# A recurrence kernel with a planned instruction order: an opening loaded in another order, with fewer filler products, a drain in place of a copy, and new planner numbers

## The chip, the cores and the metric

The kernel runs on one core of one Trainium2 chip. The metric is device time in microseconds (us) of one execution of the whole program. Besides TensorE (PE, with its weight loads as PEld), VectorE (DVE), ScalarE (ACT) and GpSimd (POOL) the core has SyncE (SP), which here issues nearly all DMAs, in order.

## The reference

Three stages follow one another. The first is a gated recurrence over 768 steps for 4 batches of 8 heads of 48, the other two mix the result by token and by channel.

```python
f = 1.0 / (1.0 + np.exp(-f_logit))
for t in range(S):
    state = f[:, :, t, :, None] * state + np.einsum('bhd,bhe->bhde', k[:, :, t], v[:, :, t])
    y[:, :, t] = np.einsum('bhd,bhde->bhe', q[:, :, t], state)
...
h = gelu_tanh(x @ w_in); u, v = halves of h
v_n = layernorm(v) * g_ln
v_s = np.einsum('ts,bsd->btd', w_sg, v_n) + b_sg[None, :, None]
x = x + (u * v_s) @ w_out
...
theta = x @ w_theta
y = einsum('ts,bsd->btd', w_tok_r, x * cos(theta)) + einsum('ts,bsd->btd', w_tok_i, x * sin(theta))
u = x + y
out = u + np.maximum(u @ w_ch, 0.0)
```

## The kernel before

The recurrence is cut into chunks of 64 tokens. For each batch the 768 tokens are two halves of 384, and each half has four units of two heads. The last unit of a half is put together from rows of the first three by small DMAs (`qkv3<-qkv0` and so on), so it can start only when those three have been scaled.

A half begins with the logits: ACT makes the gate from them, DVE runs a scan along the tokens, ACT makes the inverse of the running product. For batch 0 this is done in three parts of 384 columns, one for each of the first three units; for the later batches in one piece of 1152. GpSimd fills the scan's second operand (`seed`) and clears the last unit's tile by memsets. Then DVE scales K and Q of each unit (`scaled`). A unit (`unit`) has, on PE: three transposes of K (L822), updates and scores (L834, L843), the product inside a chunk (`inner`, L925), and the product with the state carried from earlier chunks (`carried`, L980; later batches do both in one, L940). Between them DVE masks the scores (`am`) and chains six small state steps (L871 to L880), with ACT scaling some of them (L885). ACT then copies the result to `y` (L911), and SP moves it into `xst` (L902), from which the dense part reads.

In batch 0 the first of the `carried` products reads its second block of state from spare columns of `am`; ACT puts it there by a copy (L972) that waits for the state.

The dense part of the first batch begins with plain fp32 products (`mm1`, L1014) on weights that DVE and ACT decode from 64-bit inputs (L534 to L537, `early`). Later products are three fp32r products each (`mm3`, L1002 to L1004). Batch 0's dense part is interleaved with batch 1's recurrence, and so on.

The order on every engine comes from a planner (`Plan.schedule`). It plays the operations through with costs written into the code, picks among those that are ready the one with the smallest due time (`vt`), and emits the instructions in that order; each engine then runs its list strictly in order. Constants at the top set due times: `LATE` says by when batch 1's recurrence is spread over batch 0's dense part, `U_AT` when a part of the first weights is due, `EVEN` and `ODD` when weights are decoded for later. Where the planner sees PE without work before `WARM_TO`, it puts in filler products on `ident` (L1382); how many is fixed when the program is built. On the chip they run in PE's list like any other product: 26 products are 52 records in the trace, since each fp32 product shows as two pieces.

Of the kernel before, what the change touches and what calls it, by code (L numbers as in the profile page):

```python
# [8 lines left out]
F32 = mybir.dt.float32  # L9
# [8 lines left out]
P = 128  # L18
# [41 lines left out]
EVEN, ODD = (0.05, 0.5), (0.9, 0.4)  # L60
# [3 lines left out]
LATE = 75.0  # L64
HF0, HF1, V_AT, U_AT, DENSE = (-60.0, -38.0), (-44.0, -16.0), -46.0, -24.0, -35.0
# [3 lines left out]
YQ = "SP"  # L69
MQ = "SP"  # L70
# [7 lines left out]
TICK = 10.24 / 3  # L78
DMA_SLACK = 1.0
# [60 lines left out]
class Plan:  # L140
# [63 lines left out]
    def schedule(self):  # L204
# [4 lines left out]
        free = {e: 0.0 for e in LAT}  # L209
        ticks = {}  # L210
# [39 lines left out]
        def run(a, dur, left):  # L250

            c, i = left / dur, int(a / TICK + 1e-9)
            while left > 1e-6:
                rate = c if ticks.get(i - 1, 0) >= 3060 else c / 2
                n = min(left, rate * ((i + 1) * TICK - a))
                ticks[i] = ticks.get(i, 0) + n
                left, a, i = left - n, a + n / rate, i + 1
            return a
# [99 lines left out]
def body(tc, ctx, att, lat, qkv, flog, w_in, g_ln, w_sgT, b_sg, w_out, w_theta, w_rT, w_iT, w_ch, out):  # L358
# [37 lines left out]
    gate = const.tile([P, 1], F32, name="gate")  # L396
    halfpi = fill("halfpi", math.pi / 2)
# [113 lines left out]
    def a1(n):  # L511
        return 0.1 + n * 0.00081
# [157 lines left out]
    first, ends = Buf(), []  # L670
# [12 lines left out]
    def half(pl, g, b, hf, xst, carry, vt, step):  # L683
# [15 lines left out]
        later = [first] if b else []  # L699
        for p, (t, root) in enumerate(tiles):  # L700
            for p0, p1 in groups:
                if p0 == p:
                    dma(
                        pl, eng, P * (p1 - p0) * TH * 4,
                        lambda gp=slice(p0, p1): q[eng].dma_start(f.t[:, gp], flog[b, hf][:, gp]), later, wp=fp[p0:p1],
                    )
            if p == NT:
                moved, vb, clear = (Buf(of=root) for _ in range(3))
                pl.op("POOL", 0.1 + QKE * 0.0008, lambda t=t: nc.gpsimd.memset(t.t[:, :QKE], 0.0), w=[clear], vt=vt)
# [11 lines left out]
        for p0, p1 in groups:  # L721
            gp, fs, ss, n = slice(p0, p1), fp[p0:p1], sp[p0:p1], (p1 - p0) * TH
            if b == 0:

                pl.op("POOL", 0.1 + n * 0.0008, lambda gp=gp: nc.gpsimd.memset(seed.t[:, gp], 2.0**62), w=ss)
# [11 lines left out]
                pl.op("DVE", 0.03 + n * 0.00214, scan, r=ss, w=fs)  # L737
                pl.op("ACT", a1(n), lambda gp=gp: A(seed.t[:, gp], f.t[:, gp], AF.Ln), r=fs, w=ss, table="L")
# [66 lines left out]
    def unit(pl, g, b, hf, p, be, bb, t, parts, xst, carry):  # L805
# [42 lines left out]
        if before:  # L848
            r, w, dur, fn = before
            pl.op("PE", 0.25 + 0.1 * nu + dur - 0.12, lambda fn=fn: (fn(), scores()), r=[kb, qb, vb, kt, *r], w=[ps, *w], small=True)  # L850
            carry.pop("out")()
        else:
            pl.op("PE", 0.25 + 0.1 * nu, scores, r=[kb, qb, vb, kt], w=[ps], small=True)
# [76 lines left out]
        if fused:  # L930
# [27 lines left out]
            if hf == 1 and p == NP - 1:  # L958
                r, w, dur, fn = both_
                pl.op("PE", dur, fn, r=r, w=w, small=True)  # L960
# [5 lines left out]
        def apart():  # L966
            pl.op("PE", 0.5, inner, r=[vb, am], w=[ps], small=True)
            late = range(1 - hf, 2 * NC2)
            turn = [(c, j) for c in late for j in range(2)]
            c0 = late[0]  # L970
            behind = lambda: am.t[wide[1], 1, (NC2 - 1) * HP : (NC2 - 1) * HP + D]
            pl.op("ACT", 0.2, lambda: nc.scalar.copy(behind()[:D], S[c0][0]()[rows[1]]), r=[S[c0][1]], w=[am])  # L972
            turn.remove((c0, 1))
            turn.insert(0, (c0, 1))

            def carried():
                for c, j in turn:
                    i, a = halves[c]
                    moved = (c, j) == turn[0]
                    nc.tensor.matmul(  # L980
                        score(a, i)[rows[j]], behind()[:D] if moved else S[c][0]()[rows[j]], Q()[rows[j], tok(i, a)], start=False,
                        stop=i == NC2 - 1,
                    )

            pl.op("PE", 0.134 * len(late), carried, r=[qb, *(S[c][1] for c in late), am], w=[ps], small=True)
# [631 lines left out]
```

## Time and profile before

| what | value |
|---|---|
| runs | 592.37, 595.15, 598.02 us; median 595.15 |
| profiled execution, its own time | 594.94 us |
| its span, first to last instruction | 593.2 us |
| busy share of the span | PE 97%, PEld 89%, DVE 80%, ACT 63%, POOL 4% |
| chain that ended last | PE 72%, DVE 11%, ACT 8%, DMA 5% |

The span is 1.7 us less than the execution's time. The profiled execution lies within 0.3 us of the median. A busy engine is not always one at work that the result needs: in the first 36 us much of PE's busy time is filler products. The last matmul begins 586.58 us after the span's start; what follows is one residual step and the last stores.

### The profile page before, as it was taken

What the parts mean: (1) busy time and instruction counts of PE and PEld (TensorE: products, weight loads), DVE (VectorE), ACT (ScalarE), POOL (GpSimd) and SP (SyncE); (2) the same over time, 40 slices, a digit from 0 to 9 for tenths busy, and PEclk for the clock granted to TensorE, in tenths of its full rate; (3) what the DMA queues carried; (4) which work ended last, traced back from release to release, by engine and by line L of the source; (5) the groups of instructions that cost most, each with busy time, mean ns of one, the idle gap of its engine ahead of it and who ended that gap; (6) DMA issues with size and microseconds to landing.
All of it is one profiled execution on the core that took longest, in us unless ns stands there. A gap on an engine that the chain in (4) does not pass through costs nothing.

```text
span 593.2 us, 14971 instructions
## 1 busy us (share of the span) xinstructions
PE 572.7 (97%) x5767; PEld 528.7 (89%) x5767; DVE 473.8 (80%) x1127; ACT 374.0 (63%) x828; POOL 24.8 (4%) x38
## 2 busy tenths in 40 slices
PE   8889999989999999999999999999999999999995
PEld 8646687978799989999999998999999999999995
DVE  5987789999789998699886777999968459898542
ACT  5869998569795668957488335785344249553410
POOL 3002000011001010000000000000000000000000
PEclk9999999999999999999999999999999999999999
DMA  8669574878787799787899898366788745548612
GB/s 284 177 190 306 190 216 139 283 221 251 233 278 255 255 286 329 229 247 208 275 319 328 286 330 310 125 211 231 247 273 265 249 142 158 162 135 252 187 41 85
DMA packets 61295, 136.26 MB, mean 230 GB/s; under 512 B 8096, under 2 KB 28320, under 8 KB 61216
## 3 DMA queue, kind: packets, MB, share of 16 engines
q1 hardware_dynamic: 61216, 135.23, 70.5%
q8 instruction: 47, 0.77, 0.6%
q14 instruction: 32, 0.26, 0.1%
HBM read 93.90 MB, written 34.21 MB: 216 GB/s over the span
## 4 chain that ended last, share of the span: by engine, by line
PE 72%; DVE 11%; ACT 8%; DMA 5%; issue 2%; SPq 1%; POOL 0%; DVEq 0%; ACTq 0%; POOLq 0%
PE mm L1002 16%; PE mm L1004 15%; PE mm L1003 15%; PE lmm L1004 5%; PE lmm L1002 5%; PE lmm L1003 5%; PE mm L1382 2%; DMA xst<-y 2%; PE at L940 2%; ACT L346 2%; PE at L925 1%; PE at L843 1%; PE at L822 1%; PE at L834 1%; DVE tmp L1083 1%
## 5 line engine op out<-in xcount | busy, mean ns | idle before, releaser
L1002 PE MATMUL mm<-st,ar 128*128 128x384 f32 x192 | 67.0, 349 | 0.9 <-ACT tmp L1204 0.6
L1004 PE MATMUL mm<-st,ar 128*128 128x384 f32 x192 | 64.5, 336 | 0.2 <-DVE ar L1238 0.2
L1003 PE MATMUL mm<-st,ar 128*128 128x384 f32 x192 | 64.2, 334 | 0.0
L1036 ACT CAST early<-xst 128x384 fp32r<-128x384 f32 x42 | 21.4, 511 | 30.6 <-DVE xst L1041 23.2
L1002 PEld LDWEIGHTS mm<-st,ar 128*128 128x128 f32 x192 | 36.0, 188 | 2.8 <-ACT tmp L1204 0.9
L1296 ACT CAST wout<-ar 128x384 fp32r<-128x384 f32 x48 | 24.2, 511 | 19.5 <-PE lmm L1003 9.6
L1004 PEld LDWEIGHTS mm<-st,ar 128*128 128x128 f32 x192 | 36.0, 188 | 0.5 <-DVE ar L1238 0.5
L1003 PEld LDWEIGHTS mm<-st,ar 128*128 128x128 f32 x192 | 36.1, 188 | 0.4 <-issue 0.2
L1002 PE MATMUL mm<-ar,wout 128*128 128x384 f32 x96 | 33.7, 351 | 1.7 <-DVE tmp L1128 1.3
L1002 PE MATMUL mm<-early,win 128*128 128x384 f32 x102 | 35.1, 345 | 0.0
L1004 PE MATMUL mm<-early,win 128*128 128x384 f32 x102 | 34.2, 336 | 0.0
L1003 PE MATMUL mm<-early,win 128*128 128x384 f32 x102 | 34.2, 335 | 0.0
L1003 PE MATMUL mm<-ar,wout 128*128 128x384 f32 x96 | 32.5, 338 | 0.9 <-DVE ar L1025 0.9
L1004 PE MATMUL mm<-ar,wout 128*128 128x384 f32 x96 | 32.2, 336 | 0.0
L1297 DVE TENSOR_TENSOR wout<-ar,wout 128x384 fp32r<-128x384 f32 x48 | 25.5, 551 | 7.3 <-ACT wout L1296 7.2
L1002 PE MATMUL mm<-win,early 128*128 128x512 f32 (+1 forms) x78 | 30.8, 394 | 0.0
L1004 PE MATMUL mm<-win,early 128*128 128x512 f32 (+1 forms) x78 | 29.4, 376 | 0.3 <-DVE early L1037 0.3
L1003 PE MATMUL mm<-win,early 128*128 128x512 f32 (+1 forms) x78 | 29.3, 375 | 0.0
L1041 DVE TENSOR_TENSOR xst<-xst,mm 128x384 f32<-128x384 f32 x42 | 22.5, 548 | 7.9 <-PE mm L1004 7.7
L346 ACT ACT_TABLE_LOAD x19 | 24.4, 1283 | 1.1 <-PEq L1609 0.8
L1041 DVE TENSOR_TENSOR xst<-xst,lmm 128x384 f32<-128x384 f32 x30 | 15.7, 549 | 11.8 <-PE lmm L1004 11.8
L1037 DVE TENSOR_TENSOR early<-xst,early 128x384 fp32r<-128x384 f32 x42 | 22.4, 551 | 2.2 <-ACT early L1036 2.1
(304 smaller groups left out, 1812.8 us busy)
## 6 DMA issues: line engine op xcount, KB each, us to landing
st<-scratch SPq DMA_DIRECT2D x76, 384.0 KB, 4.0
scratch<-wt SPq DMA_DIRECT2D x48, 384.0 KB, 4.1
lst<-scratch SPq DMA_DIRECT2D x44, 384.0 KB, 3.8
qkv<-in_qkv SPq DMA_DIRECT2D x21, 538.0 KB, 5.6
scratch<-st SPq DMA_DIRECT2D x12, 384.0 KB, 3.6
raw<-in_w_rT SPq DMA_DIRECT2D x12, 384.0 KB, 6.0
raw<-in_w_iT SPq DMA_DIRECT2D x12, 384.0 KB, 5.3
out<-xst SPq DMA_DIRECT2D x24, 192.0 KB, 2.2
```

The costliest lines, as they stand in the source:

```text
L346: self.nc.scalar.preload_act_table_set(SETS[load])
L822: nc.tensor.transpose(ps.t[:, 0, c], K()[:, c], ident)
L940: nc.tensor.matmul(o[rows[j]], state_[rows[j]], Q()[rows[j], tok(i, a)], start=False, stop=i == NC2 - 1 and a == 1,)
L1002: nc.tensor.matmul(o, h0, h1, start=start, stop=False, skip_group_check=more)
L1003: nc.tensor.matmul(o, h0, l1, start=False, stop=False, skip_group_check=more)
L1004: nc.tensor.matmul(o, l0, h1, start=False, stop=stop, skip_group_check=more)
L1036: pl.op("ACT", a1(TH), lambda: nc.scalar.copy(Xh(), T()), [src], [hi])
L1037: pl.op("DVE", v1(TH), lambda: V.tensor_sub(Xl(), T(), Xh().bitcast(F32)), [src, hi], [lo])
L1041: pl.op("DVE", v1(TH), lambda: V.tensor_add(T(), T(), ps.t[:, :TH]), [ps], [xst[hf].parts[k]])
L1296: pl.op("ACT", a1(TH), lambda: nc.scalar.copy(f.t[:, 0], st()), [sb], [hi])
L1297: pl.op("DVE", v1(TH), lambda: V.tensor_sub(f.t[:, 1], st(), f.t[:, 0].bitcast(F32)), [sb, hi], [lo])
L1382: nc.tensor.matmul(g.mm.tiles[i][:, :P], ident, ident, start=True, stop=True)
```

## The change

The opening (batch 0, first half) issues the first two parts of the logits ahead of the first Q/K/V tile, instead of one. GpSimd's memsets for the last unit's tile and for the second half wait for a one-column copy (`opened`) that reads the end of the first scan. The planner is told that PE starts at 0.8 us and that its first two clock windows are at half rate, so it puts in fewer filler products. In batch 0 a drain on PE ahead of all the `carried` products takes the place of the copy on ACT and of the reordering that went with it. Five numbers of the planner change, and two costs of small products.

```diff
-EVEN, ODD = (0.05, 0.5), (0.9, 0.4)
+EVEN, ODD = (0.05, 0.5), (0.8, 0.6)
...
-LATE = 75.0
-HF0, HF1, V_AT, U_AT, DENSE = (-60.0, -38.0), (-44.0, -16.0), -46.0, -24.0, -35.0
+LATE = 70.0
+HF0, HF1, V_AT, U_AT, DENSE = (-60.0, -38.0), (-44.0, -16.0), -46.0, -31.0, -35.0
...
+F_FIRST = 2
...
+COLD, PE_FROM = 2, 0.8
...
+        free["PE"] = PE_FROM
...
-                rate = c if ticks.get(i - 1, 0) >= 3060 else c / 2
+                rate = c if i >= COLD and ticks.get(i - 1, 0) >= 3060 else c / 2
...
+    opened = const.tile([P, 1], F32, name="opened")
...
-    first, ends = Buf(), []
+    first, go, ends = Buf(), Buf(), []
...
+        def clearing(t, clear, r=()):
+            pl.op("POOL", 0.1 + QKE * 0.0008, lambda: nc.gpsimd.memset(t.t[:, :QKE], 0.0), r, [clear], vt=vt)
+
+        def loads(p0, p1, vt=None):
+            dma(pl, eng, P * (p1 - p0) * TH * 4, lambda: q[eng].dma_start(f.t[:, p0:p1], flog[b, hf][:, p0:p1]), later, wp=fp[p0:p1], vt=vt)
+
+        opening = b == 0 and hf == 0
+        if opening:
+            for i, (p0, p1) in enumerate(groups[:F_FIRST]):
+                loads(p0, p1, -200.0 + i)
...
-                pl.op("POOL", 0.1 + QKE * 0.0008, lambda t=t: nc.gpsimd.memset(t.t[:, :QKE], 0.0), w=[clear], vt=vt)
+                if not opening:
+                    clearing(t, clear, [go] if b == 0 else ())
...
-                pl.op("POOL", 0.1 + n * 0.0008, lambda gp=gp: nc.gpsimd.memset(seed.t[:, gp], 2.0**62), w=ss)
+                pl.op("POOL", 0.1 + n * 0.0008, lambda gp=gp: nc.gpsimd.memset(seed.t[:, gp], 2.0**62), [go] if hf else (), ss)
...
+                if opening and p0 == 0:
+                    pl.op("POOL", 0.1, lambda: nc.gpsimd.tensor_copy(opened, f.t[:, 0, TH - 1 :]), [fs[0]], [go])
+                    clearing(qk[NT], parts[NT][3], [go])
...
-            pl.op("PE", 0.25 + 0.1 * nu + dur - 0.12, lambda fn=fn: (fn(), scores()), r=[kb, qb, vb, kt, *r], w=[ps, *w], small=True)
+            pl.op("PE", 0.25 + 0.1 * nu + dur - 0.32, lambda fn=fn: (fn(), scores()), r=[kb, qb, vb, kt, *r], w=[ps, *w], small=True)
...
-            behind = lambda: am.t[wide[1], 1, (NC2 - 1) * HP : (NC2 - 1) * HP + D]
-            pl.op("ACT", 0.2, lambda: nc.scalar.copy(behind()[:D], S[c0][0]()[rows[1]]), r=[S[c0][1]], w=[am])
...
             def carried():
-                for c, j in turn:
+                nc.tensor.drain()
+                for c in late:
...
-            pl.op("PE", 0.134 * len(late), carried, r=[qb, *(S[c][1] for c in late), am], w=[ps], small=True)
+            pl.op("PE", 0.134 * len(late) + 0.29, carried, r=[qb, *(S[c][1] for c in late)], w=[ps], small=True)
```

Since the planner's numbers change, all lists move a little. Three places follow. The first is the head of PE's list, before and after; `mm<-ident` are the filler products, `at` the banks of a unit.

```order
L1382 MATMUL mm_103<-ident 128x128 x26
L822 MATMUL at_107<-ident,qkv_116 128x128 x3
L1382 MATMUL mm_103<-ident 128x128 x13
L834 MATMUL at_107<-qkv_116,kt_180 64x48 x12
L843 MATMUL at_107<-qkv_116 64x64 x12
```

The same head of PE's list after the change:

```order
L1391 MATMUL mm_104<-ident 128x128 x17
L837 MATMUL at_108<-ident,qkv_119 128x128 x3
L1391 MATMUL mm_104<-ident 128x128 x13
L849 MATMUL at_108<-qkv_119,kt_170 64x48 x12
L858 MATMUL at_108<-qkv_119 64x64 x12
```

There are nine products fewer ahead of the first transposes, and as many as before between them and the first updates. The second place is PE's list where the third unit (`qkv_131` before, `qkv_127` after) ends and the dense products on `early` begin, before and after.

```order
L925 MATMUL at_107<-am_445,qkv_131 64x64 x12
L1014 MATMUL mm_103<-early_249,xst_0_381 128x512
L980 MATMUL at_107<-qkv_131,am_445 48x64
L980 MATMUL at_107<-qkv_131,s_443 48x64 x9
L1014 MATMUL mm_104<-early_249,xst_0_381 128x512
L1014 MATMUL mm_105<-early_249,xst_0_381 128x512
```

The same place of PE's list after the change:

```order
L940 MATMUL at_108<-am_432,qkv_127 64x64 x12
L990 MATMUL at_108<-qkv_127,s_430 48x64 x10
L1023 MATMUL mm_104<-early_242,xst_0_373 128x512
L1023 MATMUL mm_105<-early_242,xst_0_373 128x512
L1023 MATMUL mm_106<-early_242,xst_0_373 128x512
```

The `carried` products now follow `inner` at once, ahead of the first dense product. The third place is ACT's list at the first half of batch 1 (`f_817` before, `f_848` after), with its table loads, before and after; L756 and L757 (after: L771 and L772) are the logarithm and the exponential of the gate, L1065 (L1074) is a gelu.

```order
L346 ACT_TABLE_LOAD
L756 ACTIVATE seed_353<-f_817 128x1152
L346 ACT_TABLE_LOAD
L1065 ACTIVATE u_1037<-mm_105 128x384
L346 ACT_TABLE_LOAD
L757 ACTIVATE seed_353<-seed_353 128x1152
L346 ACT_TABLE_LOAD
```

The same place of ACT's list after the change:

```order
L349 ACT_TABLE_LOAD
L771 ACTIVATE seed_343<-f_848 128x1152
L770 COPY bends<-f_848 128x9
L772 ACTIVATE seed_343<-seed_343 128x1152
L349 ACT_TABLE_LOAD
L1074 ACTIVATE u_1032<-mm_106 128x384
```

Two table loads are gone there; over the whole main path ACT's list has 15 where it had 19. From about a third of PE's list on, its order is the same as before but for a few rows.

## Rows read from the trace of the kernel before

**Rows 1.** Busy time by stage: PE, PEld, DVE, ACT, POOL, clock, DMA share, GB/s
```profile
14.40:35.90 21.50, 16.89 (x357) 13.01 (x357) 21.36 (x75) 17.21 (x50) 1.06 (x1) 1.00 0.70 200
...
48.00:78.00 30.00, 28.79 (x322) 19.00 (x313) 18.86 (x45) 29.72 (x62) 3.48 (x4) 1.00 0.67 230
78.00:98.00 20.00, 18.70 (x165) 14.24 (x165) 20.00 (x49) 18.80 (x39) 0.00 (x0) 1.00 0.55 179
...
120.00:160.00 40.00, 37.02 (x650) 30.87 (x645) 37.57 (x102) 32.06 (x77) 4.46 (x5) 1.00 0.77 238
160.00:300.00 140.00, 139.97 (x1969) 131.16 (x1968) 122.13 (x307) 100.31 (x219) 7.23 (x8) 1.00 0.83 262
300.00:586.00 286.00, 283.57 (x1634) 279.14 (x1633) 215.58 (x444) 146.58 (x315) 1.70 (x2) 1.00 0.67 220
```

**Rows 2.** Timeline of the opening: start, length, engine, line, tiles, idle before
```profile
1.60 8.64 PE L1382 MATMUL mm<-ident 128*128 128x128 f32 x52 [1.60 <-POOL ident masks.py:199]
...
4.49 0.74 POOL L709 MEMSET ar<- 128x772 f32 x1
4.50 0.75 DVE L730 TENSOR_SCALAR seed<-f 128x3 f32<-128x3 f32 x1 [3.45 <-ACT f L727]
...
6.58 0.51 ACT L726 ACTIVATE f<-f 128x384 f32<-128x384 f32 x1
6.78 0.17 DVE L730 TENSOR_SCALAR seed<-f 128x3 f32<-128x3 f32 x1 [0.54 <-ACT f L727]
...
7.36 0.95 DVE L735 TENSOR_TENSOR_SCAN f<-f,seed 128x384 f32<-128x384 f32 x1
...
10.08 0.49 PE L822 MATMUL at<-ident,qkv 128*128 128x128 f32 x3
10.17 0.53 DVE L781 SCALAR_TENSOR_TENSOR qkv<-f,qkv 128x384 f32<-128x384 f32 x1
...
13.40 0.56 PE L834 MATMUL at<-qkv,kt 64*64 64x48 f32 x24
...
14.40 0.21 DVE L871 COPY s<-at 128x48 f32<-128x48 f32 x1 [1.27 <-PE at L843]
```

**Rows 3.** Filler products (line 1382) alone, by stretch
```profile
1.60:7.00 5.40, 5.40 (x25) 5.40 (x26) 1.00 0.95 317
...
10.40:13.40 3.00, 3.00 (x26) 2.88 (x26) 1.00 1.04 381
```

**Rows 4.** Timeline, third unit's end and the first dense products
```profile
26.26 0.58 PE L925 MATMUL at<-am,qkv 64*64 64x64 f32 x24
...
27.99 1.10 PE L1014 MATMUL mm<-early,xst 128*128 128x512 f32 x2 [1.15 <-DVE s L880]
...
29.02 0.25 PE L980 MATMUL at<-qkv,am 48*48 48x64 f32 x1
...
29.84 0.48 ACT L911 COPY y<-at 128x384 f32<-128x384 f32 x1 [1.01 <-PE at L980]
...
35.77 1.10 PE L1014 MATMUL mm<-early,xst 128*128 128x512 f32 x2 [2.38 <-DMA xst<-y]
```

**Rows 5.** The chain of waits at the same place: start, length, what
```profile
30.34 5.17 DMA xst<-y
```

**Rows 6.** Timeline of PE: one small product, and the first on `wout`
```profile
42.89 0.22 PE L980 MATMUL at<-ar,carry 48*48 48x64 f32 x1
...
95.61 0.44 PE L1003 MATMUL mm<-ar,wout 128*128 128x384 f32 x1 [0.86 <-DVE ar L1025]
```

**Rows 7.** The copy of line 972: count, min/median/max ns, first and last start
```profile
L972 ACT COPY am<-s x4: 227/228/228, 18.2 to 35.2; 48x48 f32<-48x48 f32 x4
```

**Rows 8.** Timeline of ACT: a table load, and the gate of batch 1's second half
```profile
62.12 1.28 ACT L346 ACT_TABLE_LOAD   x1
...
84.17 1.17 ACT L742 ACTIVATE f<-f 128x1152 f32<-128x1152 f32 x1
```

**Rows 9.** Timeline of DVE: the scan of that second half
```profile
87.40 2.55 DVE L751 TENSOR_TENSOR_SCAN f<-f,seed 128x1152 f32<-128x1152 f32 x1
```

More of the change, by code (lines that the diff above doesn't have):

```diff
@@ L699, in half @@
         later = [first] if b else []
-        for p, (t, root) in enumerate(tiles):
[L701 to L706, printed above, removed]
+        def clearing(t, clear, r=()):
[6 more added lines that the diff above has]
+                loads(p0, p1, -200.0 + i)
+        for p, (t, root) in enumerate(tiles):
+            for i, (p0, p1) in enumerate(groups):
+                if p0 == p and not (opening and i < F_FIRST):
+                    loads(p0, p1)
             if p == NT:
                 moved, vb, clear = (Buf(of=root) for _ in range(3))
-                pl.op("POOL", 0.1 + QKE * 0.0008, lambda t=t: nc.gpsimd.memset(t.t[:, :QKE], 0.0), w=[clear], vt=vt)
+                if not opening:
+                    clearing(t, clear, [go] if b == 0 else ())
                 dma(pl, eng, P * VAL * 4, lambda t=t, p=p: q[eng].dma_start(t.t[:, QKE:], qkv[b, p, hf][:, QKE:]), later, wp=[vb])
@@ L959, in unit @@
                 r, w, dur, fn = both_
-                pl.op("PE", dur, fn, r=r, w=w, small=True)
+                pl.op("PE", dur - 0.26, fn, r=r, w=w, small=True)
                 out2()
@@ L968, in apart @@
             late = range(1 - hf, 2 * NC2)
-            turn = [(c, j) for c in late for j in range(2)]
-            c0 = late[0]
-            behind = lambda: am.t[wide[1], 1, (NC2 - 1) * HP : (NC2 - 1) * HP + D]
-            pl.op("ACT", 0.2, lambda: nc.scalar.copy(behind()[:D], S[c0][0]()[rows[1]]), r=[S[c0][1]], w=[am])
-            turn.remove((c0, 1))
-            turn.insert(0, (c0, 1))
             def carried():
-                for c, j in turn:
+                nc.tensor.drain()
+                for c in late:
                     i, a = halves[c]
[L979 to L983, printed above, removed]
-            pl.op("PE", 0.134 * len(late), carried, r=[qb, *(S[c][1] for c in late), am], w=[ps], small=True)
+                    for j in range(2):
+                        nc.tensor.matmul(
+                            score(a, i)[rows[j]], S[c][0]()[rows[j]], Q()[rows[j], tok(i, a)], start=False, stop=i == NC2 - 1
+                        )
+            pl.op("PE", 0.134 * len(late) + 0.29, carried, r=[qb, *(S[c][1] for c in late)], w=[ps], small=True)
             output()
```

## The prediction

> **What bounds the kernel now.** I read the busy time by stage first [rows 1]. From 160 us to the last matmul PE is busy without a break: 139.97 of 140 us, then 283.57 of 286. So whatever PE has won or lost by 160 us comes out at the end almost whole, and nothing that only relieves another engine after that can be seen. Ahead of it PE loses 1.2 us of 30 between 48 and 78 us, where ACT is busy for 29.72; 1.3 us of 20 between 78 and 98, where DVE is busy for all 20.00; and 3.0 us of 40 between 120 and 160. Of the opening the timeline tells more, since PE's busy time there is partly filler. The 52 pieces of the first filler block occupy PE until the first transposes at 10.08 us, and the block after those until 13.40 [rows 2]. From 14.40 to 35.90 DVE is busy for 21.36 of 21.50 us [rows 1]: it sets the pace there, and it began that stretch only when PE's first scores were there, after an idle of 1.27 us [rows 2]. PE then waits 2.38 us for the move of the third unit's result, until 35.77 [rows 4].
>
> **Part 1: fillers and first unit.** The filler pieces alone [rows 3] show two paces: 25 in 5.40 us up to 7.0, that is 0.216 each, and 26 in 3.00 us later, 0.115 each. The clock column reads 1.00 in both, but the ratio is that of TensorE's two levels, 1.2 and 2.4 GHz, so the pieces tell the level better here. Seventeen products are 34 pieces: 25 until 7.0, and nine at 0.115, ending at 8.05 instead of 10.08. The transposes took 0.33 us (10.08 to the next block at 10.40), and 26 pieces follow as before, 3.0 us. PE could begin the first updates at 11.4 us, 2.0 earlier than 13.40.
>
> Do K and Q come in time? DVE's first scaled Q ended at 10.17 + 0.53 = 10.70 [rows 2]. In the new order ACT makes the exponentials of the first two parts before the first part's second step, so that part comes about 0.35 us later. Against that, its first small DVE step took 0.75 us beside a GpSimd memset of 0.74 that began 0.01 us before it, and 0.17 where none ran [rows 2]; the memset is gone from there, 0.6 us. The first scan so ends some 0.25 us earlier. But DVE's list now has the third part's small step ahead of the second scan, and it waits for ACT, whose exponential of that part began at 6.58 [rows 2]; behind it comes one more step of 0.5, so the second scan begins at about 7.8 instead of 7.36. After it stand two products, the third scan and the last step of Q: 0.95 + 0.5 + 0.5 + 0.95 + 0.5 gives 11.2. That still meets PE's 11.4. Behind it DVE has two small steps and three products of 0.5 to 0.55 each until about 13.0, when the first state copy, before at 14.40, finds its scores ready. Gain 1.4 us, from there on carried by DVE, which had no idle time to give. Ends: 2.0 (PE alone decides) and 0.8, if a moved memset falls on the third part's small step and costs the same 0.6 there.
>
> A rule speaks against this part. The Trainium skill, "SBUF — State Buffer", section "Who interferes with whom", says that a DVE step in a two-port mode, such as `tensor_scalar`, and GpSimd take one port pair in turn, whole instruction by whole instruction. The trace agrees for the one collision that it shows (0.75 against 0.17 us). Since the five memsets that now wait for the first scan come to lie where the later small steps are, by this rule the part would be worth 0.8 instead of 1.4 us, and the total 593.9.
>
> **Part 2: the third unit's result.** Its `inner` was at 26.26, its `carried` stood behind a dense product that waited 1.15 us for DVE and came at 29.02 [rows 4]; ACT's copy followed at 29.84, and the move out took 5.17 us [rows 5]. Now `carried` is ahead of that product and needs no copy on ACT: up to 2.1 us earlier. ACT's list, though, has five casts of weights ahead of the copy of the result, and the move goes into a queue that is loading 1 MB of weights, so about half of it should arrive. PE's wait of 2.38 us can shrink by 0 to 2.4; I take 1.2.
>
> **Part 3: drains.** Eight copies of 0.228 us leave ACT [rows 7]. Eight drains come to PE, each with the time that a product is under way: 0.22 us for one alone [rows 6], 0.25 in the other stretch [rows 4]. The four in the first half lie where PE waits anyway. The four after 36 us are in a stretch that PE fills: 4 x 0.25 = 1.0 us lost. Ends 0 (PE waits there anyway) and 2.0 (all eight count).
>
> The Trainium skill, "TensorEngine Tiling (Array Packing)", section "Key Properties", says that changing the tiling mode drains TensorE by itself. If `inner` on 64 rows and `carried` on 48 were two modes, the drain would be free and the total 592.3; no row shows such a pause, but none excludes it.
>
> **Part 4: ACT's table loads.** Four of 1.28 us fall away [rows 8], two of them where ACT is full, as do the four later copies. PE's losses beside a full ACT are 1.2 us, so that is all that can come back, and only if DVE, which is full right after, delivers earlier as well. Its work up to the first `wout` product, which waited 0.86 us for it [rows 6], is the same in another order, with the splits of `wout` now last. I take 0, with ends of 0 and 1.2 gained.
>
> **Part 5: the planner's numbers.** They move batch 1's recurrence and the later decodes within 48 to 300 us. The later decodes lie beside a full PE: 0. For batch 1 the order can fill gaps (at most the 1.3 and 3.0 us lost) or open new ones (below). I take 0. GpSimd's memsets for the second half are needed only after 17 us and end before 10: 0.
>
> **Sum.** 1.4 + 1.2 - 1.0 = 1.6 us less. From the profiled execution's own 594.94 that is 593.3, and as its distance to the median of 595.15 is 0.2 us, I say 593.3 for the runs too.
>
> **Rivals.** (a) Everything arrives: 2.0 from the opening, 2.4 from the wait at 35.77, 1.2 beside ACT, 1.3 and 3.0 in batch 1, drains free: 9.9 less, 585.0; with half of the last three, 587.8. For it: PE has no slack later. Against it: four conditions at once. (b) Nothing arrives, since the opening is bounded by what is loaded: the memory moves as many bytes, and PE waits at 35.77 for the same moves as before, less 1.0 for drains: 595.9. Against it: DVE, not a load, is full in that stretch. (c) Slower: in the new lists ACT has the two gate steps of batch 1's second half (1.17 us each [rows 8]) ahead of the state scalings of that batch's first unit, and DVE has the scan of 2.55 us [rows 9] ahead of the steps that feed `wout`. PE takes its list in order, so it waits at that unit's state products and again at `wout`: 2.3 + 2.55 = 4.9 us, which with the 1.6 gained gives 598.2. For it: DVE is full from 78 to 98 [rows 1], and the scan was among those steps before too, one place further on. It decides if the gate's load lands after ACT's list has reached it. (d) The tiling rule: 592.3. (e) The count of fillers is a guess of the planner; if PE's clock fell again in the opening, the small products there would run at 0.216 instead of 0.115 per piece, which for the 34 to 60 pieces concerned is at most 6 us on PE, beside a DVE that is the slower one: inside the range.
>
> **How the numbers follow.** The forecast, 591 to 595, gets 0.51; (a) 0.18; (b) 0.14; (c) 0.12; (d) 0.05. The range goes from 587.8, the half of (a), to 598.2 of (c). A change of under 1%, 6 us, can't be told from none with this kernel, whose runs spread over 5.7 us. Faster by more than that, below 589.2: 0.17, all of it from (a). Slower by more, above 601.1: 0.05, the part of (c) with further waits. Within: 0.78.
>
> **What would show it.** In the new trace the first transposes should start near 8.1 us, the first updates near 11.4, the first state copy near 13.0, and the second wait for the third unit's move should end near 33 instead of 35.77. The `carried` products after 36 us should begin 0.2 to 0.3 us after the end of `inner`. PE's losses from 48 to 160 us should stay near 5.5 us. The prediction is wrong if those grow by more than 3 us, or if DVE's first idle time after 13 us shows that a load and not DVE bounds the opening.

## The result and the profile after

The changed kernel's median is 585.91 us (583.36 to 587.46, 4 runs) against 595.32 us for the kernel before, run beside it: a ratio of 0.985, with a 95% interval of 0.9805 to 0.9894. That is faster by 1.5%, below the range on record and beside the total of rival (a). The profiled execution took 584.88 us with a span of 583.1 us, 10.1 less than before. In the changed kernel L822, L834, L843, L925, L980 and L1014 of before are L837, L849, L858, L940, L990 and L1023; in the kernels below these numbers move a little again, and the tiles' names tell which line is meant.

Busy time by stage of the changed kernel (length, PE, PEld, DVE, ACT, POOL, clock, DMA share, GB/s), which answers to [rows 1]:

```profile
14.40:35.90 21.50, 18.88 (x413) 13.75 (x412) 21.27 (x75) 17.45 (x52) 1.06 (x1) 1.00 0.78 231
48.00:78.00 30.00, 29.57 (x354) 21.06 (x352) 23.29 (x48) 29.39 (x62) 3.10 (x4) 1.00 0.83 273
78.00:98.00 20.00, 19.69 (x166) 15.76 (x168) 19.84 (x49) 14.33 (x31) 0.00 (x0) 1.00 0.45 143
120.00:160.00 40.00, 40.00 (x703) 35.54 (x705) 35.09 (x93) 37.73 (x86) 3.50 (x4) 1.00 0.83 259
160.00:300.00 140.00, 138.92 (x1810) 129.24 (x1801) 122.55 (x304) 94.68 (x214) 6.26 (x7) 1.00 0.81 264
```

PE loses 0.43 us between 48 and 78, 0.31 between 78 and 98 and nothing between 120 and 160, where it lost 1.2, 1.3 and 3.0 before: 4.8 of 5.5 us are gone. From 160 to 300 it loses 1.1, where it lost nothing.

The timeline of the opening, which answers to [rows 2] (start, length, engine, line, tiles, idle before):

```profile
1.59 6.20 PE L1391 MATMUL mm<-ident 128*128 128x128 f32 x34 [1.59 <-POOL ident masks.py:199]
...
4.84 0.17 DVE L742 TENSOR_SCALAR seed<-f 128x3 f32<-128x3 f32 x1 [3.79 <-ACT f L739]
...
6.14 0.18 POOL L751 COPY opened<-f 128x1 f32<-128x1 f32 x1 [2.68 <-DVE seed L742]
...
7.39 0.52 ACT L738 ACTIVATE f<-f 128x384 f32<-128x384 f32 x1 [2.25 <-DMA f<-in_flog]
7.63 0.49 PE L837 MATMUL at<-ident,qkv 128*128 128x128 f32 x3
...
8.02 0.74 POOL L705 MEMSET ar<- 128x772 f32 x1
...
8.57 0.21 DVE L742 TENSOR_SCALAR seed<-f 128x3 f32<-128x3 f32 x1 [1.61 <-ACT f L739]
8.65 0.95 DVE L747 TENSOR_TENSOR_SCAN f<-f,seed 128x384 f32<-128x384 f32 x1
...
10.96 0.56 PE L849 MATMUL at<-qkv,kt 64*64 64x48 f32 x24
...
13.47 0.20 DVE L886 COPY s<-at 128x48 f32<-128x48 f32 x1
```

The transposes start at 7.63 and the first updates at 10.96, both 0.4 earlier than predicted. The first state copy comes at 13.47: 0.93 earlier than before, but 0.5 later than predicted. ACT waited 2.25 us for the third part of the logits, so that the second scan began at 8.65 and not at 7.8.

PE at the third unit's end and in the second half's units, and ACT's gate of batch 1's first half, all of the changed kernel; they answer to [rows 4, 6, 8]:

```profile
25.32 0.53 PE L940 MATMUL at<-am,qkv 64*64 64x64 f32 x24
25.96 0.76 PE L990 MATMUL at<-qkv,s 48*48 48x64 f32 x20
26.66 2.83 PE L1023 MATMUL mm<-early,xst 128*128 128x512 f32 x6
...
32.43 1.13 PE L1023 MATMUL mm<-early,xst 128*128 128x512 f32 x2
...
37.30 0.58 PE L940 MATMUL at<-am,ar 64*64 64x64 f32 x24
37.99 0.32 PE L990 MATMUL at<-ar,carry 48*48 48x64 f32 x4
```

```profile
57.16 1.28 ACT L349 ACT_TABLE_LOAD   x1
58.46 1.17 ACT L771 ACTIVATE seed<-f 128x1152 f32<-128x1152 f32 x1
59.53 0.19 ACT L770 COPY bends<-f 128x9 f32<-128x9 f32 x1
59.66 1.16 ACT L772 ACTIVATE seed<-seed 128x1152 f32<-128x1152 f32 x1
60.84 1.28 ACT L349 ACT_TABLE_LOAD   x1
```

PE no longer waits for the third unit's move: the product that began at 35.77 begins at 32.43, without idle time before it. `Carried` after 36 us follows 0.11 us behind the modelled end of `inner`.

Where the 10.1 us came from is told by leads. The dense products are the same work in both kernels and stand in nearly the same order, so the difference between the starts of the n-th one is what has been won by then. Counted are records of the trace, of which a plain fp32 product has two and an fp32r product one. I use three: the 31st record of the plain fp32 products (before: 55.16 us), the last of these, the 84th (94.09), and the 301st of the fp32r ones (164.79). PE has also done as many products of the recurrence by then in both (712, 908 and 1773 records). The changed kernel leads by 4.15, 5.25 and 10.34 us there, and by 10.21 at the last product. So some four of ten were won in the opening, one from 55 to 94 us, five from 94 to 165, and nothing after.

### The profile page after: what moved, and what is told of

The parts are those of the page before. It is cut to its first block, busy times and chain, and to the rows that moved or that the text cites. A ratio compares the mean times of both kernels' runs of the same rounds, so it can differ in the third digit from the quotient of the medians.

```text
span 583.1 us, 14944 instructions
## 1 busy us (share of the span) xinstructions
PE 568.3 (97%) x5747; PEld 526.8 (90%) x5747; DVE 473.2 (81%) x1127; ACT 364.4 (63%) x816; POOL 25.0 (4%) x39
## 4 chain that ended last, share of the span: by engine, by line
PE 40%; DVE 6%; DMA 3%; ACT 2%; issue 1%; SPq 0%; DVEq 0%; ACTq 0%
PE mm L1011 8%; PE mm L1013 8%; PE mm L1012 8%; PE lmm L1013 5%; PE lmm L1011 5%; PE lmm L1012 5%; DMA raw<-in_w_iT 2%; DMA scratch<-wt 1%; DVE wt L622 1%; PE mm L1128 1%; DVE tmp L1092 1%; DVE dt L635 0%; DVE xst L1050 0%; DVE ar L1145 0%; ACT tmp L1139 0%
## 5 line engine op out<-in xcount | busy, mean ns | idle before, releaser
L621 ACT CAST wt<-dt 128x384 fp32r<-128x384 f32 x25 | 12.8, 511 | 16.6 <-DMA scratch<-wt 14.1
```

The lines of the kernel that those rows point to most:

```text
L621: pl.op("ACT", a1(TH), lambda: nc.scalar.copy(w.t[:, 0], d.t), r=[d], w=[w], vt=vt + late)
```

## The experiments

My theory after the result was a correction of the prediction: the numbers, which I had taken at 0, carry what came after 48 us. The rivals were the prediction itself (numbers 0), the drain, and the two table loads that ACT was spared. The table holds all runs. Each line has the ratio to the kernel before, run beside it (its median was 595.32 us beside the changed kernel and 593.89 to 594.24 beside the others), and the leads over the profile of before, from one execution each (negative: behind). Medians and ratios decide; a lead shows where. The changed kernel itself has 4 runs and was not run beside the others; a_odd and a_nogo, within 0.4 us of it, bear its median out. The profiled execution of a_nonums, a_uat, a_tables and a_odd was the slowest of its kernel's, so their leads at the end are low.

| kernel | median us | ratio (95%) | lead at 55 | at 94 | at 165 us | at the end |
|---|---|---|---|---|---|---|
| changed kernel | 585.91 | 0.985 (0.9805-0.9894) | 4.15 | 5.25 | 10.34 | 10.21 |
| a_open: new opening only | 596.04 | 1.0023 (0.9997-1.005) | 4.22 | -0.48 | 1.53 | -1.64 |
| b_drain: drain only | 593.96 | 0.9996 (0.9971-1.002) | 2.14 | 1.88 | 3.53 | 0.85 |
| b_nums: numbers only | 593.1 | 0.998 (0.996-0.9999) | 1.19 | 1.48 | 3.83 | 4.19 |
| a_nonums: all but numbers | 597.79 | 1.0048 (1.0027-1.0068) | 3.53 | 0.82 | -3.12 | -6.40 |
| a_copy: all but the drain | 596.23 | 1.0045 (1.0018-1.0072) | 3.51 | 1.12 | -0.17 | -0.27 |
| a_tables | 589.67 | 0.9908 (0.9872-0.9945) | 3.12 | 1.40 | 6.47 | 3.41 |
| a_drains | 592.28 | 0.9967 (0.9941-0.9994) | 2.90 | 3.37 | 5.67 | 1.89 |
| a_fill26 | 586.57 | 0.9861 (0.9825-0.9898) | 3.11 | 3.57 | 8.37 | 8.88 |
| a_nogo | 586.21 | 0.9862 (0.9825-0.9899) | 4.10 | 5.13 | 9.86 | 10.51 |
| b_pair | 594.12 | 1.0022 (0.999-1.0054) | 1.25 | 2.94 | 1.97 | 2.09 |
| n_pair | 598.14 | 1.0061 (1.0036-1.0086) | 4.18 | 1.72 | -3.72 | -5.08 |
| c_pair | 596.34 | 1.004 (1.0014-1.0066) | 3.77 | 2.25 | 0.34 | -1.39 |
| a_uat | 594.05 | 0.999 (0.9968-1.0013) | 3.06 | -0.63 | -2.68 | -3.55 |
| a_u32 | 590.16 | 0.994 (0.9917-0.9962) | 4.45 | 4.14 | 6.24 | 4.64 |
| a_l71 | 589.48 | 0.9913 (0.9885-0.9941) | 4.38 | 5.22 | 8.19 | 4.89 |
| a_cost | 588.28 | 0.9908 (0.9889-0.9926) | 3.79 | 5.12 | 7.75 | 8.55 |
| a_odd | 585.52 | 0.9851 (0.983-0.9872) | 0.77 | 1.69 | 6.58 | 6.90 |
| n_uat | 591.92 | 0.9969 (0.9938-0.9999) | 4.19 | 5.05 | 2.58 | 2.64 |

### The parts by themselves

a_nonums is the changed kernel with the constants and the two costs of before; b_nums is the kernel before with those of the change:

```diff
-LATE = 70.0
+LATE = 75.0
...
-EVEN, ODD = (0.05, 0.5), (0.8, 0.6)
+EVEN, ODD = (0.05, 0.5), (0.9, 0.4)
...
-HF0, HF1, V_AT, U_AT, DENSE = (-60.0, -38.0), (-44.0, -16.0), -46.0, -31.0, -35.0
+HF0, HF1, V_AT, U_AT, DENSE = (-60.0, -38.0), (-44.0, -16.0), -46.0, -24.0, -35.0
```

> The changed kernel with the five planner numbers and the two small-product costs of before; loads, memsets, fillers and drains stay as changed. The prediction held these numbers to be worth 0: then this kernel stays within 1 us of the changed one (near 586), and the dense products lead those of before by 9 to 10 us at the end. The rival: the numbers, by way of the order of batch 1's recurrence, carry what was gained after 48 us, about 6.5 us. Then this kernel comes at 591 to 593, its lead over before is 3 to 4 us at 33 us and does not grow after that, and PE loses 2 to 3 us again between 110 and 160 us.

> The kernel before with only the changed planner numbers and the two costs. By the prediction (numbers worth 0): 594 to 596, as before. By the rival: 588 to 590, with no lead over before at 33 us and one of 5 to 7 us at 160 us.

a_copy exchanges the drain and `carried` of the change for the copy and the turned list of before, b_drain the other way round:

```diff
-                nc.tensor.drain()
-                for c in late:
...
+            pl.op("ACT", 0.2, lambda: nc.scalar.copy(behind()[:D], S[c0][0]()[rows[1]]), r=[S[c0][1]], w=[am])
+            turn.remove((c0, 1))
+            turn.insert(0, (c0, 1))
```

> The changed kernel with the copy on ScalarE and the reordered products in batch 0 in place of the drain. By the prediction's terms the drains cost 1.0 us after 36 us and the earlier products of the third unit bring 1.2: 585.5 to 586.5, no difference. A rival: the drain, by taking the copies from ScalarE and the wait from TensorE's list, is what lets the third unit's result leave earlier, and the planner's order with it: then this kernel loses 2 to 3 us by 33 us, and ends at 588 to 589.

> The kernel before with only the drain in place of the copy in batch 0. By the prediction: 594.5 to 596. By the rival of the drain: the wait for the third unit's move ends 1.5 to 2.5 us earlier than 35.77, and the total is 592 to 593.5.

a_open is a_copy with the numbers of a_nonums, so that only loads, memsets and the filler model differ from the kernel before:

```diff
+COLD, PE_FROM = 2, 0.8
+F_FIRST = 2
...
+                    clearing(qk[NT], parts[NT][3], [go])
```

> The kernel before with the changed opening alone: the two loads first, the waiting memsets, the fewer fillers; copy and planner numbers as before. Its list has the gelu between logarithm and exponential, the slow branch. By the prediction's part 1 alone: 592.5 to 594. By what the runs so far show (each half of the change without the other is 593 to 598): the first state copy is at 13.4 to 13.6 in place of 14.40, and the total is 592 to 597, since what the opening gains is lost again between 48 and 160 us.

No part gains more than 1 us by itself (593.1 to 596.0), and taking the numbers or the drain out of the whole loses all of it and more (597.8, 596.2). The third such kernel, drain and numbers without the new opening, was not run; of the opening only fillers and memsets are taken out one by one, below. So no sum of parts gives the result, and neither simple theory holds: "numbers worth 0" fails by 11.9 us, and "the numbers carry 6.5" fails too, since by themselves they bring about 1. The leads show what happens. Every kernel with the new opening but one leads by 2.9 to 4.5 us at 55 us (a_u32's 4.45 is too high: it has 44 small products of the recurrence fewer behind it there). In a_open, a_copy and a_nonums most or all of this lead is lost between 55 and 94. b_drain shows the same on a smaller scale: its wait for the third unit's move ends 2.2 us earlier than before, as the rival of the drain said, and its median does not move.

The place is seen in PE's timeline of a_open (L1029 and L995 are the change's L1023 and L990):

```profile
55.10 0.91 PE L1029 MATMUL mm<-xst,early 128*128 128x384 f32 x2
58.22 1.57 PE L1029 MATMUL mm<-early,xst 128*128 128x512 f32 x2 [2.21 <-DMA xst<-y]
...
59.96 1.28 PE L995 MATMUL at<-ar,s 48*48 48x64 f32 x20
61.17 1.36 PE L1029 MATMUL mm<-xst,early 128*128 128x384 f32 x2
```

The same place of the changed kernel, PE, and the move on SP's queue:

```profile
54.69 0.73 PE L990 MATMUL at<-ar,s 48*48 48x64 f32 x20
55.35 1.13 PE L1023 MATMUL mm<-early,xst 128*128 128x512 f32 x2
56.31 0.81 PE L1023 MATMUL mm<-xst,early 128*128 128x384 f32 x2
56.96 1.02 PE L1023 MATMUL mm<-early,xst 128*128 128x512 f32 x2
```

```profile
50.85 1.79 SPq L917 DMA_DIRECT2D xst<-y  x3
```

The dense products on `xst` need the moves of the units' results; these here are the moves of the second half's third unit (the expectation of n_pair calls them the first half's). In the changed kernel they are issued from 50.85 and take 4.6 to 5.4 us each, and the third has landed when PE comes at 56.96. In a_open ACT makes the copy `y` at 52.02 in place of 50.37, the moves go out from 52.51, and PE, which is there 4 us earlier than before, waits 2.21 us. After that wait the same kinds of products run slower: 1.57 against 1.13, 1.28 against 0.73, 1.36 against 0.81, 1.5 us in all. The granted clock of a_open is 1.00 from 56 to 58.2 us, 0.64 from 58.2 to 60 and 0.50 from 60 to 62; over 48 to 78 us it is 0.94, that of the changed kernel 1.00. So 2.2 us of waiting cost 3.7, nearly as much as the lead at 55 us. The kernel before, which came to these products 4 us later, had no such wait.

A lead at 165 us is not always kept either. From there to the last product the changed kernel loses 0.1 us of it, but a_open, b_drain, a_nonums, a_tables, a_drains and a_l71 lose 2.7 to 3.8. In a_open PE waits 1.3 us for ACT at 166 us, for example.

### Single costs, in the changed kernel's own order

These four change one thing when the instructions are emitted and leave every engine's list as it is. a_tables:

```diff
+                if b == 1 and hf == 0:
+                    nc.scalar.preload_act_table_set(SETS["G"])
+                    nc.scalar.preload_act_table_set(SETS["L"])
                 A(seed.t[:, gp], seed.t[:, gp], AF.Exp, scale=-1.0)
```

> The changed kernel, every engine's order as it is, with two more table loads on ScalarE (1.28 us each, 2.6 us together) between the logarithm and the exponential of the gate of batch 1's first half, where the kernel before had them. The prediction's part 4 took them at 0, at most 1.2 us, since TensorE loses little beside a full ScalarE: then 586 to 587. The rival: ScalarE is full from 48 to 78 us and sets when batch 1's scaled K and Q are there, so the 2.6 us come out whole or, with the waits that follow, larger: 588 to 590, and TensorE's time without work between 60 and 100 us grows by 2 us or more.

a_drains:

```diff
                 inner()
+                nc.tensor.drain()
                 for c in range(2 * NC2):
```

> The changed kernel, every engine's order as it is, with a drain between the inner and the carried products of the 24 units of batches 1 to 3 as well. It prices a drain beside a full TensorE. The prediction's price of 0.25 us each gives 24 x 0.25 = 6 us: 592. The rival, that a drain costs about the 0.1 us that the changed kernel's trace shows between the modelled end of inner and the first carried product after 36 us, gives 2.5 us: 588 to 589. A free drain (change of tiling drains anyway): 586.

a_fill26:

```diff
-                self.idle(*o)
+                self.idle(o[0] + extra, o[1])
+                extra = 0
```

> The changed kernel, every engine's order as it is, but with 26 filler products ahead of the first transposes, as before the change, in place of 17. By the prediction's part 1, TensorE comes to the first updates 1 us later than DVE has K and Q ready (the nine products are 2.0 us), and DVE carries that on: the first state copy moves from 13.47 to 14.4 or 14.5 and the end by 1 us, to 587. A rival: the opening's gain after 27 us is from the third unit's result and not from its start, and what is late by 1 us at 14 us is caught up in TensorE's wait for the move near 32: then 586, no difference.

a_nogo:

```diff
-                    pl.op("POOL", 0.1, lambda: nc.gpsimd.tensor_copy(opened, f.t[:, 0, TH - 1 :]), [fs[0]], [go])
+                    pl.op("POOL", 0.1, lambda: None, [fs[0]], [go])
```

> The changed kernel, every engine's order as it is, without the one-column copy on GpSimd that reads the end of the first scan, so that the memsets behind it run as soon as GpSimd comes to them. By the price that the trace before showed (0.75 us for a small DVE step beside a memset, 0.17 without), the first scan starts 0.6 us later, at 5.6 in place of 5.04, and the first state copy later by up to as much; the end by 0 to 0.6: 586 to 586.5. A rival: the memsets then end before DVE's later small steps, the scan of the second part is not held up, and nothing moves or 0.3 us are gained.

Two table loads cost 589.67 - 585.91 = 3.8 us, or 3.5 against a_nogo, which was run beside a_tables. From 55 to 94 us the changed kernel wins 1.1 and a_tables loses 1.7: 2.8 us, the loads' own 2.6 and little more. What waits is PE's first fp32r products, for ACT's results just behind the loads (ACT and PE of a_tables):

```profile
60.95 1.28 ACT L774 ACT_TABLE_LOAD   x1
62.24 1.28 ACT L775 ACT_TABLE_LOAD   x1
63.53 1.16 ACT L776 ACTIVATE seed<-seed 128x1152 f32<-128x1152 f32 x1
64.71 1.28 ACT L349 ACT_TABLE_LOAD   x1
```

```profile
66.55 0.44 PE L1017 MATMUL mm<-st,ar 128*128 128x384 f32 x1 [0.53 <-ACT u L1080]
69.31 0.45 PE L1017 MATMUL mm<-st,ar 128*128 128x384 f32 x1 [1.38 <-ACT tmp L1219]
```

Twenty-four drains cost 592.28 - 585.91 = 6.4 us, 0.27 each (0.25 against a_nogo): the price of part 3 was right, and the gap of 0.11 us that the timeline shows is not all of it. The starts of the products show it: in a_drains a unit's `inner` begins at 104.73 and its first `carried` at 105.42, 0.69 us later; in the changed kernel, without a drain there, 109.70 and 110.10, 0.40 us. A drain is not free here, so rival (d) falls. The trace before had the same 0.40 us (111.97 and 112.37), so the rival could have been excluded from it.

In a_fill26 the transposes start at 9.73, the updates at 13.06 and the state copy at 14.05 (PE and DVE):

```profile
9.73 0.49 PE L839 MATMUL at<-ident,qkv 128*128 128x128 f32 x3
...
13.06 0.56 PE L851 MATMUL at<-qkv,kt 64*64 64x48 f32 x24
...
14.05 0.21 DVE L888 COPY s<-at 128x48 f32<-128x48 f32 x1 [0.32 <-PE at L860]
```

So 0.58 of the 0.93 us at the first state copy are the nine fillers' and 0.35 the loads' and memsets'. At the end 0.66 us are left, less than these medians can tell from nothing. In a_nogo the memsets run from 3.41 us on, without a pause, also beside the small step (GpSimd and DVE):

```profile
4.09 1.14 POOL L737 MEMSET ar<- 128x384 f32 x3
...
4.82 0.43 DVE L742 TENSOR_SCALAR seed<-f 128x3 f32<-128x3 f32 x1 [3.77 <-ACT f L739]
...
13.52 0.20 DVE L886 COPY s<-at 128x48 f32<-128x48 f32 x1
```

The step takes 0.43 us in place of 0.17, the scan starts 0.25 later, and the state copy 0.05: the third part's load stands between. The waiting memsets are worth nothing that shows.

### The swap: the two table loads taken out of slow plans

The five kernels with a part or without one all have, as the kernel before has, the gelu between logarithm and exponential of batch 1's first half. The swap emits the exponential right behind the logarithm and leaves out the two loads:

```diff
+                A(seed.t[:, gp], f.t[:, gp], AF.Ln)
+                if b == 1 and hf == 0:
+                    A(seed.t[:, gp], seed.t[:, gp], AF.Exp, scale=-1.0)
```

> The kernel before with one swap on ScalarE: in batch 1's first half the exponential of the gate stands right behind its logarithm, ahead of the gelu that stood between them, and the two table loads of 1.28 us that the gelu made necessary are gone. All other rows of all engines stay. Theory of the table loads (two of them cost the changed kernel 3.7 us when put back): 590 to 591.5, with a lead of 2.5 to 4 us from 90 us on. The prediction's part 4 (0, at most 1.2 us): 593 to 595.

> The changed kernel with the planner numbers of before (597.8 us), with the same swap of exponential and gelu in batch 1's first half. Theory of the table loads: 3 to 4 us less, 594 to 595; what is left over the changed kernel (8 us) is then from the rest of the order, the wait of 2.6 us for the move of the first half's result near 58 us above all. Rival: the two loads are all that parts the two plans, and it comes near 588. If they are beside other waits: 597 to 598.

> The changed kernel with the copy in place of the drain (596.2 us), with the same swap. Theory of the table loads: 592.5 to 593.5. Rival: the loads are all that parts it from the changed kernel: near 587. If they lie beside other waits: 596.

All three medians stay (594.12, 598.14, 596.34): my theory of the table loads fell. In b_pair the lead does grow by 1.7 us up to 94 us, but PE loses 1.0 us of it at the first products on `wout` (PE's waits of b_pair):

```profile
93.71 0.45 PE L1017 MATMUL mm<-ar,wout 128*128 128x384 f32 x1 [1.89 <-DVE ar L1039]
```

Before, that wait was 0.86 us [rows 6]. DVE's list had not changed, but DVE was not what held it back: it is busy for 18.66 of the 20 us from 78 to 98, where it was full before [rows 1]. What ACT had saved ran into a load, that of the logits of batch 1's second half (ACT and DVE of b_pair):

```profile
82.62 1.17 ACT L748 ACTIVATE f<-f 128x1152 f32<-128x1152 f32 x1 [1.42 <-DMA f<-in_flog]
```

```profile
85.28 0.18 DVE L752 TENSOR_SCALAR seed<-f 128x9 f32<-128x9 f32 x1 [0.97 <-ACT f L749]
```

In n_pair ACT waits 2.38 us for the same load; in c_pair it does not, and why its median stays is open. So for b_pair the 0 of the prediction's part 4 comes out, but not for its reason, a full DVE. In the changed kernel's plan, where the gate of the second half begins at 72.00 us and PE's wait at `wout` is 0.31, the same loads are worth 3.5 to 3.8 us.

### One number at a time

The expectations speak of a fork: whether the planner's list has the gelu between logarithm and exponential of batch 1's first half (the slow branch) or not (the fast one). a_uat puts `U_AT` back to -24.0, a_u32 sets it to -32.0, a_l71 sets `LATE` to 71.0, a_odd puts `ODD` back, a_cost the two costs, and n_uat is a_nonums with `U_AT` at -31.0.

```diff
-HF0, HF1, V_AT, U_AT, DENSE = (-60.0, -38.0), (-44.0, -16.0), -46.0, -31.0, -35.0
+HF0, HF1, V_AT, U_AT, DENSE = (-60.0, -38.0), (-44.0, -16.0), -46.0, -24.0, -35.0
```

> The changed kernel with one planner number of before: the due time of a part of the first weights (-24 in place of -31). In its list the gelu stands again between logarithm and exponential of batch 1's first half, as in the kernel before. By the prediction (numbers worth 0): 586. By the theory of the table loads: 589 to 590, as with the two loads put back by hand. If the whole plan of 48 to 160 us hangs together and one number upsets it: 592 to 598.

```diff
-HF0, HF1, V_AT, U_AT, DENSE = (-60.0, -38.0), (-44.0, -16.0), -46.0, -31.0, -35.0
+HF0, HF1, V_AT, U_AT, DENSE = (-60.0, -38.0), (-44.0, -16.0), -46.0, -32.0, -35.0
```

> The changed kernel with the due time of the first weights' part at -32 in place of -31. The list falls into the branch where the gelu stands between logarithm and exponential of batch 1's first half (four table loads in a row there), and half of ScalarE's first 530 rows move. Theory of the fork: 592 to 597, with no lead over before left at 90 us beyond 3 us. The prediction (numbers worth 0) and any theory in which the value -31 as such matters: 586.

```diff
-LATE = 70.0
+LATE = 71.0
```

> The changed kernel with batch 1's due time at 71 in place of 70. The list stays in the branch without the gelu between, but a third of ScalarE's rows move from row 163 on. Theory of the fork: 585 to 589, with the lead at 90 us of 5 us as in the changed kernel. If every change of the order costs, not the branch: 592 or more.

```diff
-            pl.op("PE", 0.25 + 0.1 * nu + dur - 0.32, lambda fn=fn: (fn(), scores()), r=[kb, qb, vb, kt, *r], w=[ps, *w], small=True)
+            pl.op("PE", 0.25 + 0.1 * nu + dur - 0.12, lambda fn=fn: (fn(), scores()), r=[kb, qb, vb, kt, *r], w=[ps, *w], small=True)
...
-                pl.op("PE", dur - 0.26, fn, r=r, w=w, small=True)
+                pl.op("PE", dur, fn, r=r, w=w, small=True)
```

> The changed kernel with the two small-product costs of before (0.20 and 0.26 us dearer to the planner). The branch stays the fast one; rows move from 120 on. Theory of the fork: 585 to 589. If the costs are what lets the planner fill TensorE between 110 and 160 us: 589 to 592, with 1 to 3 us lost there again.

```diff
-EVEN, ODD = (0.05, 0.5), (0.8, 0.6)
+EVEN, ODD = (0.05, 0.5), (0.9, 0.4)
```

> The changed kernel with the spread of the later weights' decodes of before (0.9, 0.4 in place of 0.8, 0.6). Its list differs only from about 155 us on, where TensorE is full: 585.5 to 587 by the prediction's part 5 and by the theory of the fork. A rival, that the decodes' places decide how much is lost between 160 and 300 us: 588 or more, with a loss over the changed kernel that begins after 155 us.

For n_uat, against a_nonums:

```diff
-HF0, HF1, V_AT, U_AT, DENSE = (-60.0, -38.0), (-44.0, -16.0), -46.0, -24.0, -35.0
+HF0, HF1, V_AT, U_AT, DENSE = (-60.0, -38.0), (-44.0, -16.0), -46.0, -31.0, -35.0
```

> The changed kernel with all planner numbers and costs of before but one, the due time of the first weights' part (-31). The list is in the fast branch again. Theory that this number alone parts the slow plans from the fast ones: 586 to 590, and no wait of 2 us or more for a move at 58 to 61 us. Rival, that the numbers only work together: 592 or more.

`ODD` is worth nothing (585.52). `U_AT` alone is worth 8.1 us, and the first place where a_uat loses is the wait of a_open: a weight store (`scratch<-st`, 384 KB) and 192 KB of weights stand about the moves of the second half's third unit, which go out from 52.61 and take 8 us, and PE waits (PE of a_uat):

```profile
61.10 2.05 PE L1023 MATMUL mm<-early,xst 128*128 128x512 f32 x2 [2.66 <-DMA xst<-y]
```

Put into a_nonums, -31 takes this wait away, and the lead at 94 us is 5.05 in place of 0.82. But n_uat then loses 2.5 us between 94 and 165, where the changed kernel wins 5.1; PE's waits of n_uat from 120 to 160 us (us in total, times, longest):

```profile
PE mm L1011 <- DVE xst L1050: 1.4, 1, 1.4
PE at L837 <- ACT s L900: 1.1, 2, 0.6
PE at L837 <- DMA st<-scratch: 1.0, 1, 1.0
```

So n_uat is at 591.92: the theory that `U_AT` alone parts the plans is half right. In that stretch a_cost and a_l71 win 2.6 and 3.0 us of the 5.1 and end 2.4 and 3.6 us slower. The kernels with the changed kernel's list there, a_odd, a_tables, a_fill26 and a_nogo, win 4.7 to 5.1, whatever their lead was when they came.

A step of 1 in `U_AT` (a_u32) costs 4.2 us. It brings the gelu back between logarithm and exponential, but the fork at that place is not the whole story either: a_u32 (590.16) has it and beats n_uat, which has not, and a_l71, which has not, is hardly faster (589.48).

## Why the prediction was wrong

**Right.** The reading that PE is full after 160 us held for the changed kernel: nothing was won there, and 0.1 us lost. The opening's terms held in sum, by luck, since neither was right. The 15 profiles with the new opening (a_fill26 aside) lead by 3.8 us at 55 us in the median, but three of before's opening lists (kernel before, b_nums, b_pair) lead by 0, 1.19 and 1.25, so the profile of before was probably itself about 1.2 late, and the gain is some 2.6 us, estimated from these single executions: parts 1 and 2, 1.4 + 1.2. The price of a drain was right, 0.25 against 0.27. Rival (d), from the Trainium skill ("TensorEngine Tiling (Array Packing)", "Key Properties"), would have made it free: a_drains does not agree with the rival. The rule itself is not tested: that the 64-row and the 48-row products are two modes, no run here shows.

**Mis-sized or wrongly placed.** Of part 1, 0.93 us arrived at the first state copy, not 1.4, because the third part's load was late. Part 2's wait vanished whole, 2.38 us, but the earlier `carried` was not needed for it: a_open, which has the copy, comes to the same product at 34.01 without a wait and has the same lead at 55 us; b_drain, which has the old opening, comes at 33.53 and waits 0.38. And 2.38 us was much for the old lists: b_nums and b_pair, with the opening and the copy of before, wait 1.18 and 1.30 there. Part 1's 0.6 us for a memset on a small step was 0.26 in a_nogo. In the changed kernel a memset of 0.74 us from 8.02 runs beside the third part's small step of 0.21 at 8.57, which so costs 0.04 over its bare 0.17; the 593.9 by the rule of the Trainium skill ("SBUF — State Buffer", "Who interferes with whom") did not come, since that memset was nearly over; a_nogo and the step's 0.43 agree with the rule, at less than half of the 0.6 us. In all three traces the step ends 0.02 us after the memset beside it (before 5.25 and 5.23, a_nogo 5.25 and 5.23, changed kernel 8.78 and 8.76), so its price was what was left of the memset.

**The steps that failed** are parts 4 and 5, "I take 0". I had listed PE's losses of 1.2, 1.3 and 3.0 us as what could come back, and rival (a) added them up to 585.0; then I left them out, since a change of order could as well open new waits. 4.8 us of them came back. Put back into the changed kernel, part 4's two loads cost 3.8 us (a_tables) and part 5's numbers with the two costs 11.9 (a_nonums): neither was worth 0. Between 55 and 165 us the changed kernel won 6.2 us; the medians' difference, 8.3 to 9.4, less the opening's 2.6 says the same. The second error is in the same step: the 2.6 us of the opening were carried to the end as if the stretch from 48 to 160 us passed a lead on. a_open shows that in the old plan it doesn't; new opening and new numbers were not two terms but one plan, and "four conditions at once" were, as far as these runs go, one condition, the list. The chance of 0.18 for (a), and a range that ended at its half, came from taking them as independent. That (a)'s total of 585.0 came within 1 us is partly luck: its 4.4 us of the opening came as 2.6, its 5.5 after that as 6.2, and its drains were not free.

Rival (c) had the right kind of mechanism, a new wait at the price of some 5 us, but not in the changed kernel: waits of that kind struck kernels with a part of the change, at the moves near 58 us. Its condition, that the gate's load lands after ACT has reached it, came true in b_pair and n_pair. The changed kernel's gate of the second half begins at 72.00 us in place of 84.17 [rows 8], clear of the splits for `wout`.

**Open.** Which rows of the list give PE its 5 us between 94 and 165 us was not isolated, only that `LATE` and the costs both have a share in it and `U_AT` by itself is not enough. Single executions differ by more than the smaller terms: a_odd has the changed kernel's list up to 155 us, but in its profile PE waited 1.59 us for a move `qkv<-qkv` at 24 us, for which it did not wait in the changed kernel's, and the lead at 55 us was 0.77. Behind that wait the granted clock was 0.53 from 26 to 28 us and 0.50 from 28 to 32: what rival (e) named, a clock that falls again in the opening, in one execution. Open is also what the opening is worth in the whole plan, since drain and numbers without it were not run, and why six kernels lose some 3 us after 165 us.

## What to carry to other kernels

Where a planner sets the order, the worth of an edit is that of the whole new list: take what the bottleneck engine loses in each stretch whose order moves as that edit's upper end, give it a real chance, and look at the waits of the new list rather than at the edit. A lead won early lasts only if the next transfer that the bottleneck engine waits for comes earlier as well; look how long ahead of its reader it lands. Test each part alone and the whole without each part: here every part alone, and both kernels without a part that were run, came out at no gain, and only that showed that the parts work together. And when what an engine saves does not come out, look for the load that it now waits for, as in b_pair, before calling the next engine full.

## What the runs showed of the hardware

The wait of 2.21 us on PE in a_open was followed by products at 1.4 to 1.75 times their time, with a granted clock of 0.50 from 60 to 62 us, that is the lower of 1.2 and 2.4 GHz; it added 1.5 us to the wait. I had priced waits at their own length. Not every wait had this after it: behind the 2.38 us of the kernel before, at 35.77, the clock was 1.00 and the product took its usual 1.10 us, and so it was in a_copy behind 1.23 us at 57.98. An explicit drain between `inner` and `carried` costs 0.27 us on a full PE, more than twice the 0.11 us between their records. A DVE step of 0.17 us took 0.75, 0.43 and 0.21 us beside GpSimd memsets and ended with them each time.
